# Hashing half of the next batch's pairs with products on GpSimd and sums on VectorE instead of matmuls on TensorE

## The chip, the cores and the metric

The kernel runs on one core of a Trainium2 chip (trn2). The metric is the device time of one execution in microseconds, the median of several runs. The engines are called as in the profile: PE (TensorE), DVE (VectorE), ACT (ScalarE), POOL (GpSimd) and SP (SyncE, which here only issues DMAs).

## The reference, cut to what matters

Two layers follow each other. The first is attention in which a query sees only the keys of the same hash bucket; the bucket is given by the signs of six projections.

```python
# q, k, v: (4, 8, 768, 64) float32; proj: (64, 6)
q_bits = (einsum('bhsd,dk->bhsk', q, proj) > 0)          # likewise k_bits
q_bucket = sum(q_bits * 2 ** arange(6)); k_bucket = ...
scores = where(q_bucket[..., :, None] == k_bucket[..., None, :], q @ k.T / 8, -1e9)
attn = softmax(scores) @ v                               # then heads side by side: x, 3072 x 512
# the second layer
ffn = (gelu(x @ w_gate) * (x @ w_val)) @ w_out           # 512 -> 1536 -> 512
out = x + sigmoid(x @ w_res) * ffn
```

## The kernel before, in words

There are four batches, and in each eight heads, taken as four pairs (`p` counts pairs, 0 to 15; `side` 0 is the query, 1 the key; `hi` is the head within the pair). A batch passes through two stages. In the **attention loop** a pair has 9 chunks, so a batch has 36 slots. A slot `s` issues the scores of one chunk on PE (`scores`, L407), their exponential on ACT (L412), some matmuls of the MLP's second half of the batch before (`mlp_mm`: `rps` L458, `fps` L472), and the product with the values of the chunk two slots earlier (`values`, L381). In the **gate stage** (`gate_val`) there are twelve blocks `m`; in each, 8 matmuls for the gate and 8 for the value (L426) fill two PSUM tiles `sp` from a ring of two; ACT takes the Gelu of the first (L445) and DVE multiplies it into the second (`hh`, L446).

The mask is folded into the matmul of the scores: each row of q and k, cast to bf16 by POOL into a tile `nat` (`cast`, L184 and L186), gets its six sign bits as further columns (`bits`, L225), and a DMA transpose on SP's queue brings the whole into the layout of the matmul (`turn`, L274, tile `aug`). There are only four `nat` tiles, so a cast waits for the `turn` of the tile's last user. To find the bits, DVE transposes the raw data in 32x32 blocks into a tile `t32` (`tr`, L194), PE multiplies them by the projection (`hash_mm`, L206, float32; 16 matmuls for two pairs, in four column groups), and DVE turns the sums back into rows of tokens (`hash_tok`, L216) before the bits are set.

An output tile `av` (PSUM, ring of two, one for each head) is opened by a DVE memset of a spare row (`opened`, L347), then a PE matmul puts a small multiple of the sum of all values there (`preset`, L355, which reads `vsum` from POOL's `vals_s`, L307 to L311), and a copy spreads that row over the six others (`repeat`, L359, DVE), after which `values` may add to it. When a head is done, DVE divides by the sum (`finish`, L332 and L333), which also frees the tile for `opened` of the pair after it. The MLP's output takes two DVE operations: L476 on `fps`, and L479, which adds x (`o` and `x_tok`, both in SBUF).

All order is written out by hand; every engine executes its own instructions in the order in which the program issues them. Batch 0 has a list, `ORDER`. In batches 1 to 3, `at(s, ...)` hangs a piece behind the values of slot `s`, `pe(s, ...)` behind its scores, and `gv(b, m, ...)` behind block `m` of batch `b`'s gate stage. Beside batch `b` the pairs of batch `b + 1` are prepared: the first two, called `xs`, and the second two, `ys`, each as four (pair, side) items. Both are hashed by PE in the gate stage: `xs` behind block 0, `ys` behind block 6, with DVE's `hash_tok` and `bits` behind blocks 0 to 4 and 7 to 10. Batch 0 prepares the pairs of batch 1 in the same way from `ORDER`.

Of the kernel before, what the change touches and what calls it, by code (L numbers as in the profile page):

```python
# [9 lines left out]
FP32 = mybir.dt.float32  # L10
BF16 = mybir.dt.bfloat16
AF = mybir.ActivationFunctionType
ALU = mybir.AluOpType
# [4 lines left out]
def kernel(  # L18
# [12 lines left out]
    nc = tc.nc  # L31
# [27 lines left out]
    ld_pool = ctx.enter_context(tc.tile_pool(name="ld", bufs=4))  # L59
    ldv_pool = ctx.enter_context(tc.tile_pool(name="ldv", bufs=3))  # L60
    aug_pool = ctx.enter_context(tc.tile_pool(name="aug", bufs=4))
    t32_pool = ctx.enter_context(tc.tile_pool(name="t32", bufs=6))
    va_pool = ctx.enter_context(tc.tile_pool(name="va", bufs=4))
    e_pool = ctx.enter_context(tc.tile_pool(name="e", bufs=4))
    sm_pool = ctx.enter_context(tc.tile_pool(name="sm", bufs=2))
    sc_ps = ctx.enter_context(tc.tile_pool(name="sc_ps", bufs=2, space=PSUM))
    av_ps = ctx.enter_context(tc.tile_pool(name="av_ps", bufs=2, space=PSUM))
# [105 lines left out]
    def nat_of(x):  # L173
        return nat[(2 * x[0] + x[1]) % NN]

    def cast(p, side, eng, h0=0, h1=2):
        x = (p, side)
        scale = (1.0 / C) if side == 0 else 1.0
        sl = slice(h0 * T, h1 * T)
        dst = nat_of(x)[:, sl, 0:D]  # L180
        if eng is nc.scalar:
            nc.scalar.activation(dst, raw[x][:, sl], AF.Copy, scale=scale)
        elif side == 0:
            eng.tensor_scalar(dst, raw[x][:, sl], scale, 1.0, op0=ALU.mult, op1=ALU.mult)  # L184
        else:
            eng.tensor_copy(dst, raw[x][:, sl])  # L186

    t32, hsum, htok = {}, {}, {}

    def tr(p, side, h0=0, h1=2):  # L190
        if (p, side) not in t32:
            t32[p, side] = t32_pool.tile([P, HT, 2, 32], FP32, tag="t32", name="t32")
        sl = slice(h0 * T, h1 * T)
        nc.vector.transpose(t32[p, side][:, sl].rearrange("p c h n -> p (c h n)"),  # L194
                            raw[p, side][:, sl].rearrange("p c d -> p (c d)"))
# [48 lines left out]
                                hs[:, 1, :, 0:NBITS], 0.0, 0.5, op0=ALU.is_gt, op1=ALU.subtract)  # L244


    def hash_heads(p, dh):
        if p not in hsum:
            hsum[p] = mm_ps.tile([P, T, 32], FP32, tag="r", name="hsh")
        hs = hsum[p]  # L250
        for j in range(4):
            hi, side = divmod(j, 2)
            nc.tensor.matmul(hs[32 * j:32 * j + 32], projw[:, dh, :],  # L253
                             t32[p, side][:, hi * T:hi * T + T, dh, :],
                             start=(dh == 0), stop=(dh == 1), tile_position=(0, 32 * j))

    def tok_heads(p):
        ht = sm_pool.tile([P, T, 32], FP32, tag="hth", name="hth")
        nc.vector.transpose(ht.rearrange("p c n -> p (c n)"),
                            hsum.pop(p).rearrange("p c n -> p (c n)"))  # L260
        htok[p] = ht
# [80 lines left out]
    def opened(p, hi):  # L342
        if (p, hi) in av:
            return
        av[p, hi] = av_ps.tile([P, T + 1, D + 1], FP32, tag="av", name="av")
        if p >= HP:
            nc.vector.memset(av[p, hi][:, T, :], 0.0)  # L347

    def preset(p, hi):
        o, w = av[p, hi], vsums[p][:, hi, 0:D + 1]  # L350
        if p < HP:
            nc.tensor.matmul(o[:, 0:T, :], eps_sb, w.unsqueeze(1).to_broadcast([P, T, D + 1]),  # L352
                             start=False, stop=True, skip_group_check=True)
        else:
            nc.tensor.matmul(o[:, T, :], eps_sb, w, start=False, stop=True, skip_group_check=True)  # L355

    def repeat(p, hi):
        o = av[p, hi]
        nc.vector.tensor_copy(o[:, 0:T, :], o[:, T:T + 1, :].to_broadcast([P, T, D + 1]))  # L359

    def x_turn(b, hp):
        pt = mm_ps.tile([P, T, P], BF16, tag="f", name="pt") if b == 0 else \
# [130 lines left out]
    def at(s, *pieces):  # L493
        side_work.setdefault(s, []).extend(pieces)

    def pe(s, *pieces):
        side_pe.setdefault(s, []).extend(pieces)

    def gv(b, m, *pieces):
        gv_work.setdefault((b, m), []).extend(pieces)  # L500

    def loads(s, *xs):
        for p, what in xs:
            at(s, (lambda p=p: load_v(p)) if what == "v" else
               (lambda p=p, w=what: load(p, "qk".index(w))))


    for p in range(HP, NPAIR):
        for hi, s in enumerate((9 * p - 1, 9 * p + 4)):
            if p == HP and hi == 0:  # L510
                gv(0, 8, lambda: opened(HP, 0))
                gv(0, 9, lambda: preset(HP, 0))
                gv(0, 9, lambda: repeat(HP, 0))
                continue
            at(s - 2, lambda p=p, hi=hi: opened(p, hi))
            pe(s, lambda p=p, hi=hi: preset(p, hi))
            at(s, lambda p=p, hi=hi: repeat(p, hi))

    def hashed(ps, i0=0, i1=4):
        jobs = [(p, side) for p in ps for side in range(2)]  # L520
# [73 lines left out]
    def lay(b, m, x):  # L594
        gv(b, m, lambda: bits(*x), lambda: turn(*x))

    for b in range(B - 1):
        s0, p0 = b * NSLOT, (b + 1) * HP
        xs = [(p0 + i, side) for i in range(2) for side in range(2)]
        ys = [(p0 + 2 + i, side) for i in range(2) for side in range(2)]  # L600
        for j, (x, y) in enumerate(zip(xs, ys)):
            if b == 0:
                for z in (x, y):
                    n = "%d%s" % (z[0], "qk"[z[1]])
                    put("ld " + n, lambda z=z: load(*z))
                    put("tr " + n, lambda z=z: tr(*z))
                n = "%d%s" % (x[0], "qk"[x[1]])
                put("cast " + n, lambda x=x: cast(*x, nc.gpsimd))
                put("hash 4.%d" % j, lambda p0=p0, j=j: hashed((p0, p0 + 1), j, j + 1))
                continue  # L610
            at(s0 + 24 + 2 * j, lambda x=x: tr(*x))
            at(s0 + 25 + 2 * j, lambda x=x: cast(*x, nc.gpsimd))
            if j < 2:
                at(s0 + 32 + 2 * j, lambda y=y: tr(*y))
            loads(s0 + 2 + 4 * j, (x[0], "qk"[x[1]]))
            loads(s0 + 18 + 3 * j, (y[0], "qk"[y[1]]))
        if b > 0:
            gv(b, 0, lambda p0=p0: hashed((p0, p0 + 1)))
        gv(b, 0, lambda p0=p0: tokens((p0, p0 + 1), True))
        for m, x in zip((0, 1, 2, 4), xs):  # L620
            lay(b, m, x)
        if b > 0:
            gv(b, 3, lambda y=ys[2]: tr(*y))
            gv(b, 5, lambda y=ys[3]: tr(*y))
        for m, y in zip((5, 5, 6, 6), ys):
            gv(b, m, lambda y=y: cast(*y, nc.gpsimd))
        if b > 0:
            gv(b, 6, lambda p0=p0: hashed((p0 + 2, p0 + 3)))
        gv(b, 7, lambda p0=p0: tokens((p0 + 2, p0 + 3), True))
        for m, y in zip((7, 8, 9, 10), ys):  # L630
            lay(b, m, y)
    for p in range(HP, NPAIR):
        at(9 * p - 8, lambda p=p: vals_s(p), lambda p=p: vals_a(p))
        loads(9 * p - 20, (p, "v"))

    mlp, done = [], [0]
    NMM = T * (KM + KF)
# [134 lines left out]
```

## Time and profile before

| | us |
|---|---|
| median of 3 runs (lowest to highest) | 344.25 (344.13 to 345.43) |
| the profiled execution's own time | 344.05 |
| its span, first to last instruction | 342.3 |
| PE busy | 337.0 (98%) |
| ACT busy | 208.1 (61%) |
| DVE busy | 192.9 (56%) |
| POOL busy | 86.1 (25%) |

A row of the groups by line gives line, engine, operation, output<-input tile, shapes and count, then the busy time and the mean duration of one in ns, then the idle time of the engine just before, with what ended it. The timeline gives start, duration, engine and line. The granted TensorE clock is full in all 40 slices.

Batch 1's gate stage runs from 126.4 to 160.7 us, batch 2's from 206.7 to 241.0, batch 3's from 286.7 to 317.9; between them lie the attention loops of batches 2 and 3.

### The profile page before, as it was taken

The page shows a single profiled execution, that of the slowest core. Times are in us where ns is not written, and L with a number is a line of the kernel's source. Part 1 is how long each engine was busy: PE and PEld are TensorE (multiplying, and loading weights), DVE is VectorE, ACT ScalarE, POOL GpSimd, SP SyncE. Part 2 cuts the span into 40 slices and gives each one's busy share as a digit, 9 for nine tenths or more (in the row PEclk, how much of TensorE's full clock was granted, in tenths as well). Part 3 has the DMA queues.
Part 4 walks back from the last instruction along what each step waited for, and adds up shares of the span by engine and source line. Part 5 has one row for each costly group of instructions (what it writes and reads, how often), then busy time and mean ns, then how long its engine had stood idle before and what let it go on. Part 6 is the DMA issues. An engine that isn't in the chain of part 4 may idle for free.

```text
span 342.3 us, 7633 instructions
## 1 busy us (share of the span) xinstructions
PE 337.0 (98%) x3124; PEld 204.6 (60%) x3124; DVE 192.9 (56%) x406; ACT 208.1 (61%) x235; POOL 86.1 (25%) x165
## 2 busy tenths in 40 slices
PE   8999999999999999999999999999999999999995
PEld 5667665665666665655666665656566665665443
DVE  6878847574444876756344775747334444333343
ACT  4889973237999862325999991222999994322220
POOL 3899830370055000170054000242030000000000
PEclk9999999999999999999999999999999999999999
DMA  7979999979386523518467542725431221000012
GB/s 225 377 153 231 308 184 183 162 114 208 123 186 191 159 77 90 110 19 166 105 164 213 181 107 69 132 49 103 82 97 36 56 56 61 3 0 0 33 61 93
DMA packets 69571, 42.50 MB, mean 124 GB/s; under 512 B 47904, under 2 KB 66592, under 8 KB 69536
## 3 DMA queue, kind: packets, MB, share of 16 engines
q1 hardware_dynamic: 63120, 36.77, 42.5%
q0 software_dynamic: 6336, 5.24, 10.6%
q8 instruction: 24, 0.39, 0.5%
q14 instruction: 11, 0.09, 0.1%
q10 hardware_dynamic: 80, 0.00, 0.0%
HBM read 29.36 MB, written 6.29 MB: 104 GB/s over the span
## 4 chain that ended last, share of the span: by engine, by line
PE 94%; ACT 3%; DMA 1%; DVE 1%; issue 0%; SPq 0%; DVEq 0%; ACTq 0%
PE sp L426 37%; PE fps L472 18%; PE sp L407 17%; PE av L381 10%; PE rps L458 6%; PE hs L206 3%; ACT e L412 3%; PE pt L285 1%; DMA ld<-in_q_dram 1%; PE pt L365 1%; PE hs L235 0%; PE av L352 0%; PE hsh L253 0%; PE av L355 0%; DVE o L479 0%
## 5 line engine op out<-in xcount | busy, mean ns | idle before, releaser
L412 ACT ACTIVATE e<-sp 128x1024 bf16<-128x1024 f32 x144 | 143.6, 1026 | 13.1 <-PE sp L407 8.4
L445 ACT ACTIVATE gt<-sp 128x768 bf16<-128x768 f32 x48 | 38.9, 811 | 93.6 <-PE sp L426 93.6
L407 PE MATMUL sp<-aug,aug 71*128 71x256 bf16 (+1 forms) x384 | 85.8, 325 | 0.3 <-ACT e L412 0.2
L472 PE MATMUL fps<-wo,hh 128*128 128x512 bf16 (+2 forms) x300 | 79.3, 370 | 0.0
L446 DVE TENSOR_TENSOR hh<-gt,sp 128x768 bf16<-128x768 bf16 x48 | 45.8, 955 | 52.1 <-PE sp L426 50.0
L426 PE MATMUL sp<-x_sb,wg 128*128 128x512 bf16 (+1 forms) x384 | 70.5, 326 | 0.1
L426 PE MATMUL sp<-x_sb,wv 128*128 128x512 bf16 (+1 forms) x384 | 70.4, 326 | 0.0
L381 PEld LDWEIGHTS <-e 128*128 128x128 bf16 x1152 | 52.7, 97 | 28.9 <-issue 1.2
L381 PE MATMUL av<-va,e 128*128 128x65 bf16 x1152 | 57.6, 193 | 0.0
L426 PEld LDWEIGHTS <-wg 128*128 128x128 bf16 x384 | 37.0, 98 | 26.0 <-issue 1.8
L426 PEld LDWEIGHTS <-wv 128*128 128x128 bf16 x384 | 37.6, 98 | 24.8
L472 PEld LDWEIGHTS <-hh 128*128 128x128 bf16 x300 | 27.5, 97 | 23.2
L407 PEld LDWEIGHTS <-aug 71*128 71x128 bf16 x384 | 29.4, 97 | 10.9 <-issue 1.4
L194 DVE STREAM_TRANSPOSE t<-ld 128x768 f32<-128x768 f32 (+1 forms) x34 | 30.7, 913 | 4.1 <-DMA ld<-in_q_dram 2.2
L307 POOL TENSOR_TENSOR v<-ldv 128x384 f32<-128x384 f32 x16 | 15.9, 996 | 66.5 <-DMA ldv<-in_v_dram 66.5
L184 POOL TENSOR_SCALAR nat<-ld 128x768 bf16<-128x768 f32 x15 | 12.4, 829 | 73.5 <-DMA aug<-nat 73.5
L476 DVE SCALAR_TENSOR_TENSOR o<-th,fps 128x512 f32<-128x512 f32 (+2 forms) x25 | 16.6, 666 | 24.5 <-PE fps L472 20.1
L458 PE MATMUL rps<-wr,x_sb 128*128 128x512 bf16 x96 | 28.1, 378 | 0.0
L332 DVE RECIPROCAL rec<-av 128x6 f32<-128x6 f32 x32 | 6.2, 193 | 32.9 <-PE av L381 31.0
L359 DVE COPY av<-av 128x390 f32<-128x390 f32 x24 | 13.6, 565 | 19.3 <-PE av L355 19.2
L462 ACT ACTIVATE th<-rps 128x512 f32<-128x512 f32 x24 | 14.2, 593 | 16.5 <-PE rps L458 16.5
L225 DVE TENSOR_SCALAR nat<-htp 32x72 bf16<-32x72 f32 x96 | 21.9, 229 | 1.7
(67 smaller groups left out, 209.5 us busy)
## 6 DMA issues: line engine op xcount, KB each, us to landing
ldv<-in_v_dram SPq DMA_DIRECT2D x16, 384.0 KB, 5.1
out_dram<-o SPq DMA_DIRECT2D x23, 256.0 KB, 2.1
ld<-in_q_dram SPq DMA_DIRECT2D x15, 384.0 KB, 5.1
ld<-in_k_dram SPq DMA_DIRECT2D x15, 384.0 KB, 4.5
wg<-in_moe_w_gate_dram POOLq DMA_DIRECT2D x4, 384.0 KB, 6.8
wv<-in_moe_w_val_dram POOLq DMA_DIRECT2D x4, 384.0 KB, 6.8
wo<-in_moe_w_out_dram POOLq DMA_DIRECT2D x3, 512.0 KB, 6.1
wr<-in_moe_w_res_dram POOLq DMA_DIRECT2D x1, 512.0 KB, 11.6
```

The costliest lines, as they stand in the source:

```text
L194: nc.vector.transpose(t32[p, side][:, sl].rearrange("p c h n -> p (c h n)"), raw[p, side][:, sl].rearrange("p c d -> p (c d)"))
L225: engs[a % len(engs)].tensor_scalar(nat_of(x)[32 * a:32 * a + 32, :, D:D + NBITS], ht[32 * j:32 * j + 32, :, NBITS * a:NBITS * (a + 1)], 0 ...
L307: nc.gpsimd.tensor_add(v3, vs[:, :, 0:3, :], vs[:, :, 3:6, :])
L381: nc.tensor.matmul(av[p, hi][:, qt, :], e[:, off:off + P], va[:, hi, jt, 0:D + 1], start=first, stop=(p >= HP and jt == T - 1), skip_group ...
L407: nc.tensor.matmul(sp[:, off:off + nq * P], ks[0:KA, hi * T + jt, :], qs[0:KA, hi * T + qt0:hi * T + qt0 + nq, :], start=True, stop=True)
L412: nc.scalar.activation(e, sp, AF.Exp, scale=float(ALPHA))
L426: nc.tensor.matmul(sp[:, c0:c1], w[:, kk, bass.ts(m, P)], xs[:, kk, c0:c1], start=(kk == 0), stop=(kk == KM - 1))
L445: nc.scalar.activation(gt, sp[:, 0:S], AF.Gelu)
L446: nc.vector.tensor_mul(hh[:, m, :], gt, ps[1][:, 0:S])
L458: nc.tensor.matmul(rps, x_sb[b][:, kk, t, :], wr[:, kk, :], start=(kk == 0), stop=(kk == KM - 1))
L472: nc.tensor.matmul(fps[:, cs], hh[:, m, bass.ts(t, P)], wo[:, m, cs], start=(m == 0), stop=(m == KF - 1))
L476: nc.vector.scalar_tensor_tensor(o[:, cs], th[:, cs], 1.0, fps[:, cs], op0=ALU.add, op1=ALU.mult)
```

## The change

Beside batches 1 and 2, the `ys` are no longer hashed by PE. For each of the four items, POOL forms the products of two token columns with all six projection vectors in one instruction (`multiply`, output 128 x 2 x 6 x 64, float32, both inputs read with a repeated dimension), and DVE sums each over the 64 (`add_up`, a reduction from 768 numbers to 12 in each partition). Six such pairs make one item; `bits_val` then sets its bits in one DVE instruction. The products take a ring of two tiles (`t2`) out of the six that `t32` had. The projection is spread once over all partitions (`spread_proj`). `tr`, `hash_mm`, `hash_tok` and four `bits` for each of these items go.

Two of the eight `repeat` copies of a batch (`(p % 4, hi)` of `(0, 0)` and `(2, 0)`) move from DVE to ACT. The pieces beside batches 1 to 3 have new places from a table `PLACE`: a whole part below 36 is a slot, 36 to 47 a gate block, 48 and above a slot of the batch after; a fraction below .5 means behind the scores (as `pe`), from .5 on behind the values (as `at`). Batch 0's own order stays, except for which `t32` tile each transpose writes (`TRING`).

```diff
-    t32_pool = ctx.enter_context(tc.tile_pool(name="t32", bufs=6))
+    t32_pool = ctx.enter_context(tc.tile_pool(name="t32", bufs=2))
+    TRING = (0, 1, 2, 0, 1, 2, 1, 0, 0, 1, None, None, 0, 1)
-            t32[p, side] = t32_pool.tile([P, HT, 2, 32], FP32, tag="t32", name="t32")
+            t32[p, side] = t32_pool.tile([P, HT, 2, 32], FP32, tag="t%d" % TRING[p], name="t32")
+    def spread_proj():
+        pb = sm_pool.tile([P, D, NBITS], FP32, tag="ht", name="pb")
+        nc.sync.dma_start(pb, proj.partition_broadcast(P))
+        nc.gpsimd.tensor_copy(projt, pb.rearrange("p d n -> p n d"))
+    def multiply(x, t):
+        pr = t32_pool.tile([P, 2, NBITS, D], FP32, tag="t2", name="pr")
+        nc.gpsimd.tensor_tensor(pr, raw[x][:, t:t + 2].unsqueeze(2).to_broadcast([P, 2, NBITS, D]),
+                                projt.unsqueeze(1).to_broadcast([P, 2, NBITS, D]), op=ALU.mult)
+        prod[x, t] = pr
+    def add_up(x, t):
...
+        nc.vector.tensor_reduce(hval[x][:, t:t + 2, :], prod.pop((x, t)),
+                                axis=mybir.AxisListType.X, op=ALU.add)
+    def bits_val(x):
+        nc.vector.tensor_scalar(nat_of(x)[:, :, D:D + NBITS], hval.pop(x), 0.0, 0.5,
+                                op0=ALU.is_gt, op1=ALU.subtract)
     def repeat(p, hi):
+        if (p % HP, hi) in ((0, 0), (2, 0)):
+            nc.scalar.activation(o[:, 0:T, :], o[:, T:T + 1, :].to_broadcast([P, T, D + 1]), AF.Copy)
+    PLACE = {
...
+        "tr x": (14.5, 26.02, 15.5, 25.04),
+        "cast x": (23.54, 6.04, 23.02, 25.5),
+        "bits x": (36.56, 36.6, 45.5, 37.52),
+        "turn x": (39.54, 37.5, 47.52, 44.58),
+        "cast y": (46.52, 38.52, 50.06, 62.02),
+        "bits y": (43.5, 43.54, 56.54, 70.06),
+        "turn y": (56.02, 47.5, 59.04, 70.52),
+        "mul y0": (22.04, 23.52, 31.02, 33.02, 33.5, 35.5),
+        "mul y1": (36.58, 38.5, 39.5, 41.5, 41.54, 42.52),
+        "mul y2": (42.54, 44.52, 49.02, 49.5, 50.04, 51.5),
+        "mul y3": (53.02, 57.02, 57.5, 58.5, 59.5, 61.52),
+        "add y0": (24.02, 29.5, 32.02, 33.06, 35.02, 37.54),
+        "add y1": (38.54, 39.52, 40.5, 41.52, 42.5, 43.52),
+        "add y2": (44.5, 46.5, 49.52, 50.02, 52.5, 53.5),
+        "add y3": (56.5, 57.52, 59.06, 61.5, 64.04, 67.02),
+        "open 0": (36.52, 7.02, 15.52, 25.02),
+        "open 1": (0.04, 11.02, 19.5, 29.02),
+        "preset 0": (44.56, 8.56, 18.04, 27.04),
+        "repeat 0": (46.54, 8.58, 18.5, 28.02),
+        "repeat 1": (5.04, 12.5, 23.04, 33.04),
...
     for b in range(B - 1):
...
-        if b > 0:
-            gv(b, 6, lambda p0=p0: hashed((p0 + 2, p0 + 3)))
```

## The prediction, made before the changed kernel was run

> **What bounds the kernel now.** First the page: its busy times, then the chain that ended last.
>
> ```profile
> PE 337.0 (98%) x3124; PEld 204.6 (60%) x3124; DVE 192.9 (56%) x406; ACT 208.1 (61%) x235; POOL 86.1 (25%) x165
> ...
> PE 94%; ACT 3%; DMA 1%; DVE 1%; issue 0%; SPq 0%; DVEq 0%; ACTq 0%
> ```
>
> PE is the bound almost everywhere; POOL has three quarters of its time free. Next the same chain in order of time, where the change acts:
>
> ```profile
> 126.43 2.60 PE sp L426 x16
> 129.03 1.44 PE hs L206 x32
> 130.47 15.71 PE sp L426 x96
> 146.18 1.44 PE hs L206 x32
> 147.61 13.11 PE sp L426 x80
> ```
>
> From 126.43 to 160.72 PE has no gap, and each hash is 1.44 us on the path (129.03 to 130.47, 146.18 to 147.61). Batch 2 has the same at 209.28 and 226.42. The groups kept apart by shape give the prices of what comes and goes:
>
> ```profile
> L194 DVE STREAM_TRANSPOSE t<-ld 128x768 f32<-128x768 f32 x30 | 28.6, 960 | 2.9 <-PE hs L206 1.9 <-DMA ld<-in_q_dram 1.0
> ...
> L479 DVE SCALAR_TENSOR_TENSOR o<-o,x_tok 128x512 f32<-128x512 f32 x23 | 17.1, 745 | 0.8
> ...
> L307 POOL TENSOR_TENSOR v<-ldv 128x384 f32<-128x384 f32 x16 | 15.9, 996 | 66.5 <-DMA ldv<-in_v_dram 66.5
> ...
> L309 POOL TENSOR_TENSOR v<-v 128x128 f32<-128x128 f32 x16 | 7.3, 454 | 1.3
> ```
>
> Last the timeline of POOL and of DVE at 177 us, for what the two do to each other:
>
> ```profile
> 177.25 0.83 POOL L184 TENSOR_SCALAR nat<-ld 128x768 bf16<-128x768 f32 x1
> ...
> 177.33 1.29 DVE L479 SCALAR_TENSOR_TENSOR o<-o,x_tok 128x512 f32<-128x512 f32 x1
> ...
> 178.03 1.27 POOL L186 CAST nat<-ld 128x768 bf16<-128x768 f32 x1
> ```
>
> L479 takes 0.69 us when POOL is quiet; here it began inside POOL's 0.83 and took 1.29, and POOL's next cast took 1.27 in place of 0.82. They took turns. Of all DVE groups only L479, with both inputs in SBUF, is ever stretched so: L446 stays at 0.95 and L194 at 0.97 beside a busy POOL.
>
> **What it removes.** Two hashes of 1.44 us, both on the path: 2.88 us. From DVE, beside each of the two batches, four transposes of 0.96 (two in late slots, two in gate blocks), one `hash_tok` of 0.59 and sixteen `bits` of 0.23; none held PE, so that is worth nothing by itself.
>
> **What it adds.** 48 products on POOL. The two rows of L307 and L309 lie on a line of (0.996 - 0.454) / 256 = 2.12 ns an element; 768 elements are 0.454 + 640 x 0.00212 = 1.81 us. Nearest rows on both sides: the cast L299, one input of 768, 0.85 us, is the floor. The 32x72 `bits` on POOL (L225, twelve short runs) takes 0.469, 0.23 more than the casts' line gives for 72 elements (0.50 for 384, 0.83 for 768), so 19 ns a run; with that for some 10 to 20 more runs a product would be 2.0 to 2.2. I take 1.8, since L307 is the same operation with two inputs. All 48 are 87 us, spread over two batch times of some 77 us.
>
> 48 sums on DVE. No reduction is in the trace. The nearest are L194 and L446, 768 elements in 0.96, some 0.88 from start to start when nothing is waited for; below, 0.69 (L476, 512 elements); above, 1.29 (L479 when it waits for POOL). I take 0.95, 46 us in all, where 20 go (16.2 of the hash, 3.4 of six copies).
>
> The Trainium skill (GPSIMD Engine Reference, "Performance versus the Vector engine") speaks against the change: elementwise work with two inputs belongs on VectorE, which is about twice as fast. The trace agrees in size: L479's slope between 128x128 (0.292) and 128x512 (0.69 undisturbed) is 1.04 ns an element, half of POOL's 2.12. By the rule the products would go to DVE at 0.292 + 640 x 0.00104 = 0.96 each, 23 us more of DVE in each batch; as the walk below shows, DVE has not that much left, so the rule does not decide here.
>
> Six `repeat` copies go from DVE (0.57) to ACT, about 0.5 each (L367, 256 columns, 0.38; L462, 512, 0.59). ACT is busy 25.0 of 27.0 us in the first slots of batch 2, and one copy there still fits; a slip of under 0.9 us of an exponential is hidden by the second `sp` tile. `spread_proj` is one DMA and one POOL copy (0.5 to 1.0) where POOL sat idle 16.4 us: nothing. If that cover were gone, 1.0 us of POOL.
>
> In batch 0 the transpose of 6q now waits for the hash of 4q, which is read until 44.2: DVE does it at 44.25 where it did it at 41.39, so 7k and 6k come 0.96 later. What follows is head (3,1)'s division, before which DVE sat idle 1.02 us for PE. Covered; otherwise up to 1.0.
>
> **The waits it adds.** Every sum waits on DVE for its product, and behind it wait `hh`, `finish`, `opened` and `repeat`, on which PE waits; every third product waits on POOL for a sum (ring of two), and behind it wait casts and the sums of the values.
>
> *Gate blocks* (2.60 us each). DVE: `hh` 0.95 and one sum 0.95, at most another 0.95 of `bits` (block 1): 2.85, less two overlaps of 0.08: 2.7. PE needs `hh`'s tile again after the next gate half, so the slack is 1.30 - 0.95 = 0.35: held. POOL: 8 products in the stage, 14.5, two casts, `vals` 3.0: 19 of 31 us. The cast behind the second product waits for the `turn` issued behind block 1: bits done at 133.0, landing 3.7 later, 136.7; POOL arrives at 137.7. Covered by 1.0.
>
> *Slots 0 to 22 of the batch after* are the tight stretch: DVE has there 10 sums 9.5, L476 and L479 thrice 4.2, four divisions 3.0, two transposes 1.9, copies and memsets 2.2: 20.8 of 26.5 us. I walk it from the end of block 11. Sums 2 and 3 of item y2 end at 2.7; product 4 started when sum 2 had freed its tile, 2.0, and ends 3.8; sum 4 ends 4.7; `repeat` 5.2. POOL: cast 3.7 to 4.5, product 5 to 6.2, y3's first to 8.0. L476 runs at 6.9, when `fps` is complete; L479 could start at 7.6 and takes its turn after the product, until 8.5. Sum 5 until 9.4, division 10.1, memset for (9,0) 10.3. PE reaches that `preset` at 10.6: slack 0.3. The same way on: three more sums, L479 again waiting for a product until 17.8, sum 18.7, transpose, division, transpose, memset for (10,0) 21.3; PE wants it at 21.6: slack 0.3. POOL's sum of values for pair 11 comes at 31.1, wanted 32.1; the `repeat` for (11,0) 34.7, wanted 34.8.
>
> So with these prices nothing stops PE, but slacks of 0.1 to 0.3 us after eight products in a row will not all hold: I allow 0.4 for both batches together. Sum against the profiled execution: 344.05 - 2.88 + 0.4 = 341.6. That execution lies 0.2 under the median of the runs.
>
> **The rivals.** *Part of it is given back* (0.22): a product of 1.9 to 2.05. The memset at slot 18 comes after some eight products in turn, so each 0.1 makes it 0.8 later, less 0.3 of slack, in two batches: 1.9 to 2.05 costs about 1.0 to 3.4, and gives 342.2 to 344.6. For it: the two inputs are read in up to twelve runs. Against: L307's straight line has the same start, 0.18, as the casts, which have twelve runs of 64.
>
> *POOL becomes the bound* (0.20, the slower side). At 2.2 a product the memset of slot 18 comes 8 x 0.4 - 0.3 = 2.9 late in each of two batches, and POOL's queue to pair 11's sum of values (11 products) costs another 1.5 in batch 2: 344.05 - 2.88 + 7.3 = 348.5. It decides from about 2.1 us a product (2 x (2.4 - 0.3) + 0.5 = 4.7, less 2.88). The same would come of sums that take turns with the products as L479 does, at once some 0.5 each. Against: L194, one input from SBUF, is never stretched.
>
> *The matmuls' time is not freed*, since PE then waits for `hh`: block 7 would start 1.44 sooner, but DVE also loses `hash_tok` there. I see no more than 0.1 in it, so it gets no chance of its own.
>
> **How the numbers follow.** The main case, 0.58, has 341.0 to 342.4. About 0.5% (1.7 us) is what a measurement of this kernel can tell from no change; faster by that is below 342.5. Taking in the first rival and half of the second, the range is 340.8 to 346.0. Faster 0.58, same 0.22, slower 0.20.
>
> **What would show it.** L206 with 160 records, not 224; gate stages of batches 1 and 2 of 32.9 us, not 34.3; a POOL row of 48 tensor-tensors near 1.8, POOL near 175 us busy; a DVE row of 48 reductions near 0.95; L479's mean up to about 0.85. Right would be that the attention loops of batches 2 and 3 keep their length within 0.5. Wrong would be products of 2.1 or more, reductions stretched beside POOL, or PE idle before L355 or L381 in those loops, waiting for DVE's memset or copy.

## The result, and the profile after

The changed kernel takes 342.73 us (median of 4 runs, 342.28 to 342.96) against 344.50 for the kernel before beside it (4 runs, 344.13 to 345.43): a ratio of 0.9943, 95% interval 0.9919 to 0.9967. It is faster by 0.57%, little more than the 0.5% that the prediction gives as what can be told from no change. Its profiled execution took 342.96 us, span 341.3.

From the page of the kernel after, its busy times, the engines' shares of the chain that ended last, and three groups:

```profile
PE 332.9 (98%) x3014; PEld 203.5 (60%) x3060; DVE 221.1 (65%) x414; ACT 210.0 (62%) x241; POOL 174.5 (51%) x214
...
PE 90%; DVE 4%; ACT 3%; issue 2%; POOL 0%; DVEq 0%; ACTq 0%; POOLq 0%
...
L259 POOL TENSOR_TENSOR pr<-ld,projt 128x768 f32<-128x768 f32 x48 | 86.4, 1811 | 41.2 <-DVE hv L266 41.0
...
L266 DVE TENSOR_REDUCE hv<-pr 128x12 f32<-128x768 f32 x48 | 44.6, 936 | 4.7 <-POOL pr L259 4.6
...
L509 DVE SCALAR_TENSOR_TENSOR o<-o,x_tok 128x512 f32<-128x512 f32 (+2 forms) x25 | 22.3, 894 | 0.9
```

A product takes 1.811 us and a sum 0.936. PE is still 98% busy, but DVE's share of the chain is 4% where it was 1%: somewhere DVE has become what PE waits for. L509 is the old L479 (L506 is L476, L476 is L446, L208 is L206, L374 and L382 are `opened` and `preset`).

Where the time went is read best by stage. The table is worked out from the start times in PE's timeline. "Start" is the beginning of the first hash in the last quarter of batch 0's attention loop. A gate stage runs from its first matmul to the first `rps` of the loop that follows it, a loop from there to the next gate stage. Loops 2 and 3 follow the gate stages of batches 1 and 2; loop 1 is the one before.

| profile of | start | loop 1 | gate 1 | loop 2 | gate 2 | loop 3 | gate 3 | span |
|---|---|---|---|---|---|---|---|---|
| before | 39.87 | 45.37 | 34.72 | 45.52 | 34.73 | 45.33 | 31.20 | 342.3 |
| after | 40.41 | 45.47 | 33.57 | 45.86 | 33.57 | 45.64 | 31.20 | 341.3 |
| e4, no products or sums | 40.41 | 45.34 | 33.21 | 45.34 | 33.21 | 45.34 | 31.21 | 339.6 |
| e1, bits and turn moved | 40.40 | 45.47 | 33.21 | 47.03 | 33.21 | 45.70 | 31.20 | 342.2 |
| e2, a sum later | 40.43 | 45.47 | 33.57 | 46.70 | 33.58 | 45.78 | 31.20 | 342.3 |
| e3, write-back into PSUM | 40.45 | 45.35 | 33.57 | 45.34 | 33.57 | 45.34 | 31.20 | 340.4 |
| e5, slower products | 39.66 | 45.47 | 33.57 | 47.25 | 33.58 | 45.92 | 31.21 | 342.2 |
| e6, copies on DVE | 39.94 | 45.35 | 33.57 | 45.85 | 33.57 | 45.63 | 31.20 | 340.6 |
| e7, products on DVE | 39.78 | 46.35 | 36.67 | 54.09 | 36.17 | 49.60 | 31.20 | 359.4 |
| e8, bits moved alone | 39.71 | 45.46 | 33.21 | 45.86 | 33.22 | 45.63 | 31.20 | 339.8 |
| e9, e3 and e8 | 40.71 | 45.35 | 33.21 | 45.34 | 33.21 | 45.34 | 31.20 | 339.9 |
| e10, before with e3's edit | 40.68 | 45.37 | 34.72 | 45.37 | 34.72 | 45.33 | 31.20 | 343.0 |
| before, second profile | 40.72 | 45.43 | 34.72 | 45.78 | 34.72 | 45.34 | 31.20 | 343.5 |

From before to after the two gate stages lose 1.15 and 1.16 us, the three loops grow by 0.10, 0.34 and 0.31: 1.56 less in all. The start differs by 0.54 the other way, so the spans show only 1.0; the medians show 1.77. The second profile of the kernel before (last row) has loop 2 at 45.78 instead of 45.52. Against that one the loops grow by 0.04, 0.08 and 0.30, and the stages lose 1.88 in all. The medians lie between the two. The row without products is the floor: 33.21 for a gate stage and 45.34 for a loop. So the change leaves two things on the table: 0.36 in each gate stage, and 0.13, 0.52 and 0.30 in the loops.

**The gate stage.** The chain of the kernel after, in order of time:

```profile
129.67 1.44 PE hs L208 x32
...
133.92 0.95 DVE hh L476
...
136.91 0.96 DVE hh L476
...
137.92 2.11 PE sp L456 x12
```

The one hash that is left stands alone; behind it PE's run of blocks breaks off, and the chain goes through DVE, from one `hh` to the next. DVE's timeline there, in the kernel after (start, duration, what, and in brackets the idle time before with its releaser):

```profile
133.92 0.95 DVE L476 TENSOR_TENSOR hh<-gt,sp 128x768 bf16<-128x768 bf16 x1 [0.22 <-PE sp L456]
134.91 0.98 DVE L227 TENSOR_SCALAR nat<-htp 32x72 bf16<-32x72 f32 x4
135.92 0.95 DVE L266 TENSOR_REDUCE hv<-pr 128x12 f32<-128x768 f32 x1
136.91 0.95 DVE L476 TENSOR_TENSOR hh<-gt,sp 128x768 bf16<-128x768 bf16 x1
137.78 0.94 DVE L266 TENSOR_REDUCE hv<-pr 128x12 f32<-128x768 f32 x1
```

Block 1 has `hh`, four `bits` and a sum, one behind the other with no time between them: 2.99 us from `hh` to `hh`, where a block of PE is 2.60. PE's timeline shows what it costs:

```profile
136.25 1.46 PE L456 MATMUL sp<-x_sb,wg 128*128 128x512 bf16 x8
137.92 1.46 PE L456 MATMUL sp<-x_sb,wv 128*128 128x512 bf16 x8 [0.20 <-DVE hh L476]
```

Eight matmuls take 1.30 from start to start when nothing waits; here it is 1.67, so 0.37 are lost.

**The loops.** Loops 2 and 3 run level with the kernel before up to slot 8 and then lose 0.30 at slot 9, at the `preset` of head (9,0) or (13,0). DVE's timeline of the kernel after, ahead of it:

```profile
167.14 0.69 DVE L506 SCALAR_TENSOR_TENSOR o<-th,fps 128x512 f32<-128x512 f32 x1 [1.58 <-ACT e L442]
167.86 1.13 DVE L509 SCALAR_TENSOR_TENSOR o<-o,x_tok 128x512 f32<-128x512 f32 x1
168.91 0.94 DVE L266 TENSOR_REDUCE hv<-pr 128x12 f32<-128x768 f32 x1
...
170.63 0.11 DVE L374 MEMSET av<- 128x65 f32 x1
```

and POOL's, at the same time:

```profile
164.85 3.58 POOL L259 TENSOR_TENSOR pr<-ld,projt 128x768 f32<-128x768 f32 x2
```

L509 could have begun to work at 167.86 and been done in 0.69; it waits for the second product, which ends at 168.43, and takes 1.13. Everything behind it up to the memset (L374) shifts with it. PE has this in its timeline of the kernel after:

```profile
170.43 0.41 PE L411 MATMUL av<-va,e 128*128 128x65 bf16 x8
...
171.02 0.59 PE L437 MATMUL sp<-aug,aug 71*128 71x512 bf16 x2
```

From the values (L411) to the next scores (L437) it is 0.59 us, with the `preset` between them. The view of PE's waits does not list this one; only the comparison with a run that lacks it (e3 below: 0.27) shows it.

In loop 2 another 0.22 go in slot 29, where the values of head (11,0) wait for its copy (L389). The chain of the kernel after, in order of time, passes through DVE there:

```profile
193.65 1.15 DVE o L509
194.80 0.49 DVE av L389
```

It is L509 again, 1.15 us long, this time beside POOL's casts and not beside a product. 0.30 and 0.22 are loop 2's 0.52 above the floor; loop 3 has the 0.30 alone.

Loop 1 loses 0.12 at the same slot, but not by L509, which takes its 0.69 there. L506 ahead of it begins late: 32.51 us after the start of the loop, where it is 32.15 in e4. What held it the profile does not show. The late start is also in loop 1 of e1, e2, e5 and e8, and it is missing from loop 1 of e3, e4, e6 and e9.

### The profile page after: what moved, and what is told of

It reads as the page before. It is cut to its first block, busy times and chain, and to the rows that moved or that the text cites. A ratio compares the mean times of both kernels' runs of the same rounds, so it can differ in the third digit from the quotient of the medians.

```text
span 341.3 us, 7515 instructions
## 1 busy us (share of the span) xinstructions
PE 332.9 (98%) x3014; PEld 203.5 (60%) x3060; DVE 221.1 (65%) x414; ACT 210.0 (62%) x241; POOL 174.5 (51%) x214
## 4 chain that ended last, share of the span: by engine, by line
PE 90%; DVE 4%; ACT 3%; issue 2%; POOL 0%; DVEq 0%; ACTq 0%; POOLq 0%
PE sp L456 34%; PE fps L502 17%; PE sp L437 17%; PE av L411 10%; PE rps L488 6%; ACT e L442 3%; PE hs L208 2%; PE hs L237 1%; DVE hh L476 1%; PE wps L151 1%; PE pt L312 1%; DVE o L509 1%; DVE nat L227 1%; PE pt L395 1%; DVE t L196 1%
## 5 line engine op out<-in xcount | busy, mean ns | idle before, releaser
L259 POOL TENSOR_TENSOR pr<-ld,projt 128x768 f32<-128x768 f32 x48 | 86.4, 1811 | 41.2 <-DVE hv L266 41.0
L437 PE MATMUL sp<-aug,aug 71*128 71x256 bf16 (+1 forms) x384 | 85.8, 325 | 0.4 <-ACT e L442 0.2
L476 DVE TENSOR_TENSOR hh<-gt,sp 128x768 bf16<-128x768 bf16 x48 | 45.8, 954 | 46.1 <-PE sp L456 44.0
L502 PE MATMUL fps<-wo,hh 128*128 128x512 bf16 (+2 forms) x278 | 74.6, 369 | 1.1
L456 PE MATMUL sp<-x_sb,wv 128*128 128x256 bf16 (+1 forms) x374 | 69.9, 324 | 0.9 <-DVE hh L476 0.4
L456 PE MATMUL sp<-x_sb,wg 128*128 128x256 bf16 (+1 forms) x376 | 70.0, 325 | 0.5
L411 PEld LDWEIGHTS <-e 128*128 128x128 bf16 x1152 | 52.7, 97 | 29.3 <-issue 1.8
L411 PE MATMUL av<-va,e 128*128 128x65 bf16 x1152 | 57.6, 193 | 0.1
L266 DVE TENSOR_REDUCE hv<-pr 128x12 f32<-128x768 f32 x48 | 44.6, 936 | 4.7 <-POOL pr L259 4.6
L437 PEld LDWEIGHTS <-aug 71*128 71x128 bf16 x384 | 29.4, 97 | 11.1 <-issue 1.7
L506 DVE SCALAR_TENSOR_TENSOR o<-th,fps 128x512 f32<-128x512 f32 (+2 forms) x25 | 16.6, 666 | 25.2 <-PE fps L502 17.1
L488 PE MATMUL rps<-wr,x_sb 128*128 128x512 bf16 x90 | 26.4, 378 | 0.4
L196 DVE STREAM_TRANSPOSE t<-ld 128x768 f32<-128x768 f32 (+1 forms) x26 | 22.7, 895 | 4.3 <-PE hs L208 2.7
L509 DVE SCALAR_TENSOR_TENSOR o<-o,x_tok 128x512 f32<-128x512 f32 (+2 forms) x25 | 22.3, 894 | 0.9
L185 POOL TENSOR_SCALAR nat<-ld 128x768 bf16<-128x768 f32 x15 | 13.7, 911 | 14.7 <-DMA aug<-nat 14.7
L187 POOL CAST nat<-ld 128x768 bf16<-128x768 f32 (+1 forms) x15 | 12.9, 862 | 13.9 <-DMA aug<-nat 6.8
```

The lines of the kernel that those rows point to most:

```text
L259: nc.gpsimd.tensor_tensor(pr, raw[x][:, t:t + 2].unsqueeze(2).to_broadcast([P, 2, NBITS, D]), projt.unsqueeze(1).to_broadcast([P, 2, NBITS ...
L266: nc.vector.tensor_reduce(hval[x][:, t:t + 2, :], prod.pop((x, t)), axis=mybir.AxisListType.X, op=ALU.add)
L411: nc.tensor.matmul(av[p, hi][:, qt, :], e[:, off:off + P], va[:, hi, jt, 0:D + 1], start=first, stop=(p >= HP and jt == T - 1), skip_group ...
L437: nc.tensor.matmul(sp[:, off:off + nq * P], ks[0:KA, hi * T + jt, :], qs[0:KA, hi * T + qt0:hi * T + qt0 + nq, :], start=True, stop=True)
L456: nc.tensor.matmul(sp[:, c0:c1], w[:, kk, bass.ts(m, P)], xs[:, kk, c0:c1], start=(kk == 0), stop=(kk == KM - 1))
L476: nc.vector.tensor_mul(hh[:, m, :], gt, ps[1][:, 0:S])
```

## The experiments

Theory: the hash is gone from the path in full, products and sums have the predicted lengths, and what is given back are two waits for DVE, each with one cause: block 1 of the gate stages is overfull, and L509 takes turns with POOL at the tight places of the loops. Rivals: POOL itself is the bound; a cost at the start; the moved copies.

**e4: what the change costs in all.** `multiply` and `add_up` return at once, and the signs come from a tile of zeros.

```diff
     def multiply(x, t):
+        return
...
     def add_up(x, t):
+        hval[x] = hzero
+        return
```

> Leaves out all 48 products and 48 sums (the signs of these four items are set from a tile of zeros); the places, the copies on ACT and the missing hashes are the changed kernel's. Theory (all that is lost of the 2.88 us is DVE's and POOL's added work): the gate stages are 33.27, the loops of batches 2 and 3 as long as before or shorter, and the time is about 2.9 us under the kernel before, near 341.5. Rival (the new places or the copies on ACT cost something by themselves): it stays above 342.2.

Measured: 340.86 us (340.54 to 341.32), ratio 0.990 (0.9882 to 0.9918). This is the floor row of the table. One hash is worth 34.72 - 33.21 = 1.51 us of the path (its row has 1.44), and the products and sums cost 342.73 - 340.86 = 1.9 us together by the medians, 1.67 by the stages.

**e1: emptying block 1, with the turn.** Two of the four `bits` of item x3 go from block 1 to block 9, and its `turn` from block 8 to block 9.

```diff
-        "bits x": (36.56, 36.6, 45.5, 37.52),
-        "turn x": (39.54, 37.5, 47.52, 44.58),
+        "bits x": (36.56, 36.6, 45.5, 37.52, 45.54),
+        "turn x": (39.54, 37.5, 47.52, 45.58),
...
+                place(b, "bits x", 3, lambda x=x: bits_half(*x, 0))
+                place(b, "bits x", 4, lambda x=x: bits_half(*x, 1))
```

> Half of the bits of one item (the first two pairs' last key) move from behind gate block 1 to behind block 9, so that DVE has there half a set of bits and a sum. Theory (the gate stages of batches 1 and 2 lose 0.30 us each because hh, four bits and a sum take 2.99 us behind block 1): each of these gate stages goes from 33.57 to about 33.27 us, the hash's 1.44 us less than before in full; the attention loops keep 45.86 and 45.64; the run is about 0.6 us under the changed kernel, near 342.1. Rival (the 0.30 us comes from something other than DVE's row there): the gate stages keep 33.57.

Measured: 343.83 us (343.17 to 344.02), ratio 0.9978 (0.9969 to 0.9988), 1.1 slower than the changed kernel. The gate stages do fall to 33.21. But loop 2 is 47.03: at slot 9 it loses 1.2 us more than the kernel after. POOL's timeline and DVE's in this run:

```profile
164.87 0.83 POOL L185 TENSOR_SCALAR nat<-ld 128x768 bf16<-128x768 f32 x1 [1.15 <-DMA aug<-nat]
```

```profile
167.50 2.30 DVE L517 SCALAR_TENSOR_TENSOR o<-o,x_tok 128x512 f32<-128x512 f32 x1
```

The later `turn` keeps a `nat` tile longer; POOL's cast waits 1.15 us for it, the two products behind the cast end at 169.25 instead of 168.43, and the add with x (L517 here) waits for both of them: 2.30 us. The block was the cause of the gate stall, and the edit brought a second effect with it. So it was done again without the `turn`. (In the cuts of both edits, `bits_half` sets two of an item's four `bits`.)

**e8: emptying block 1, without the turn.** The two `bits` go from block 1 to block 2.

```diff
-        "bits x": (36.56, 36.6, 45.5, 37.52),
+        "bits x": (36.56, 36.6, 45.5, 37.52, 38.53),
...
+                place(b, "bits x", 3, lambda x=x: bits_half(*x, 0))
+                place(b, "bits x", 4, lambda x=x: bits_half(*x, 1))
```

> Half of item x3's bits moves from gate block 1 to gate block 2; its turn stays where it is (in e1_split_bits it went one block later, and POOL's cast behind it then waited 1.15 us more). The rest is the changed kernel. Theory: block 1's stall of 0.36 goes, gate stages 33.21 in place of 33.57, and the chain to slot 9 runs along with PE (hh paces the sums), so loops 2 and 3 stay at 45.9 and 45.6 within 0.15: 342.73 - 0.7 = 342.0. Rival (the chain to slot 9 is paced by POOL's products, not by PE): what the gate stage gains, the memset of slot 9 gives back, loops 46.2 and 46.0, time 342.7.

Measured: 341.84 us (341.56 to 342.05), ratio 0.9913 (0.9898 to 0.9927). DVE's timeline in the same block:

```profile
133.23 0.95 DVE L484 TENSOR_TENSOR hh<-gt,sp 128x768 bf16<-128x768 bf16 x1 [0.22 <-PE sp L464]
...
135.83 0.95 DVE L484 TENSOR_TENSOR hh<-gt,sp 128x768 bf16<-128x768 bf16 x1
```

From `hh` to `hh` it is 2.60, the gate stages are 33.21 and 33.22, and the loops stay as they were. The rival, that the memset of slot 9 would give the gain back, fell: the sums behind `hh` move along with PE.

**e2: one sum out of the way of slot 9.**

```diff
-        "add y2": (44.5, 46.5, 49.52, 50.02, 52.5, 53.5),
+        "add y2": (44.5, 46.5, 49.52, 50.02, 52.5, 55.04),
```

> The sum that stands on DVE ahead of the division and the memset for the second pair's first head moves behind that memset. Theory (the attention loops of batches 2 and 3 lose 0.30 us at slot 9 because that memset comes too late): the memset comes 0.9 us sooner, PE waits at slot 9 no more, the loops go from 45.86 and 45.64 to about 45.55 and 45.35; but the product that waits for the moved sum, and all after it, come up to 1.2 us later, so that some may be lost again at slot 18. Rival (the loops are longer for another reason, such as the exponentials or the matmuls themselves): the stall at slot 9 goes or stays, and the loops keep their length.

Measured: 343.93 us (343.19 to 344.41), ratio 0.9985 (0.9974 to 0.9995). The wait at slot 9 is gone (0.31), and two others have come, at the `preset` of (9,1) and of (10,0). By the start times of the scores behind them they cost 0.45 and 0.68, so loop 2 is 0.84 longer than in the kernel after. The sum is not all that came later. DVE's timeline of this run, behind the memset of slot 9:

```profile
171.48 1.17 DVE L270 TENSOR_SCALAR nat<-hv 128x72 bf16<-128x72 f32 x1
```

In the kernel after this `bits_val` takes 0.33 there. Here the product behind the moved sum is later too (170.79 to 172.60), and `bits_val` lasts until that product ends, which costs DVE 0.84. How the loss divides between the moved sum and this second effect was not tried apart; shown is that moving one piece within the stretch from slot 9 to slot 18 was no remedy. In loop 3, where no next batch is prepared, the gain at slot 9 and the loss at the next `preset` leave 0.14.

**e3: L509 without its second SBUF input.** L506 writes its result back into its PSUM tile, and the add with x reads it there.

```diff
-                nc.vector.scalar_tensor_tensor(o[:, cs], th[:, cs], 1.0, fps[:, cs],
+                nc.vector.scalar_tensor_tensor(fps[:, cs], th[:, cs], 1.0, fps[:, cs],
...
-                nc.vector.scalar_tensor_tensor(o3, o3, 0.5, x_tok[b][:, k0:k1, t, :],
+                f3 = fps[:, cs].rearrange("p (k n) -> p k n", n=P)
+                nc.vector.scalar_tensor_tensor(o3, f3, 0.5, x_tok[b][:, k0:k1, t, :],
```

> The MLP's first DVE operation writes back into its PSUM tile and the second reads it from there, so that the second has one input in SBUF instead of two; everything else is the changed kernel's. Theory (L509 takes turns with POOL's products because both its inputs are in SBUF, and that is what makes the memset for slot 9 late): the second operation's mean goes from 0.935 to about 0.70, none is stretched beside a product, the loops of batches 2 and 3 lose nothing at slot 9 and go to about 45.55 and 45.35; the gate stages keep 33.57; about 0.6 us less. Rival (any DVE operation that reads SBUF beside a product is stretched): the mean stays above 0.85 and the loops keep their length.

Measured: 342.07 us (341.73 to 342.27), ratio 0.9933 (0.9913 to 0.9953). All three loops are at the floor (45.35, 45.34, 45.34) with the products still there; loop 1 is there in e6 too, without this edit, so its 0.12 is not counted for it. DVE's timeline before slot 9, the groups by shape, and PE's timeline at slot 9 in this run:

```profile
167.78 0.69 DVE L510 SCALAR_TENSOR_TENSOR o<-fps,x_tok 128x512 f32<-128x512 f32 x1
```

```profile
L510 DVE SCALAR_TENSOR_TENSOR o<-fps,x_tok 128x512 f32<-128x512 f32 x23 | 15.9, 691 | 0.8
```

```profile
170.35 0.41 PE L411 MATMUL av<-va,e 128*128 128x65 bf16 x8
...
170.62 0.60 PE L437 MATMUL sp<-aug,aug 71*128 71x512 bf16 x2
```

The same add at the same place, beside the same products, takes 0.69 instead of 1.13; all 23 have a mean of 0.691, where L509's 512-wide form has 0.935 in the kernel after. From L411 to L437 it is 0.27 instead of 0.59. The Trainium skill (SBUF — State Buffer, "Who interferes with whom") says that a VectorE instruction with two SBUF inputs contends with a GpSimd instruction that reads SBUF, under an exclusive lock, and that one with at most one SBUF input does not, outside the modes that use both ports. The two rows, 0.935 and 0.691, agree with it.

**e10: the same edit without products.** The kernel before, with e3's edit and nothing else.

> The kernel before with the write-back into PSUM of e3_psum_stt and nothing else: tells whether that edit gains by itself or only against the products. Theory (L509 is stretched by the products): the loops before stood at 45.37, 45.52 and 45.33 against 45.34 without products, so at most 0.2 to 0.3 is there to be had; the time stays within 0.4 of 344.5. Rival (a general gain of the edit): loop 2 and others shorter than 45.34, time 343.5 or less.

Measured: 344.27 us (343.75 to 344.90), ratio 0.9989 (0.9980 to 0.9999). Loop 2 goes from 45.52 to 45.37, and no other stage moves. What it mends there stands in DVE's timeline of the first profile of before, and then of the second:

```profile
185.60 0.99 DVE L479 SCALAR_TENSOR_TENSOR o<-o,x_tok 128x512 f32<-128x512 f32 x1
```

```profile
186.49 1.26 DVE L479 SCALAR_TENSOR_TENSOR o<-o,x_tok 128x512 f32<-128x512 f32 x1
```

L479 took turns with POOL's casts and sums of values ahead of the memset for (10,1) before the change too, and PE's scores behind it start 0.14 and 0.41 later than in e4. With the edit it takes 0.69 there. So the edit alone is worth 0.15 or 0.41 in these profiles and 0.4 in the medians, a tenth of a per cent. In the changed kernel this place costs nothing any more, and the edit takes away other waits: 0.30 in loop 3, which the kernel before does not lose at all, and 0.52 in loop 2. The 0.30 at slot 9 of each loop comes from the products; the 0.22 of slot 29 stands beside casts, at the new places.

**e5: slower products.** A memset of 128x128 on POOL ahead of each product.

```diff
+    idle = const.tile([P, P], BF16, name="idle")
...
     def multiply(x, t):
+        nc.gpsimd.memset(idle, 0.0)
```

> A memset of 128x128 (bf16, 0.15 to 0.25 us) goes on POOL ahead of each product; the products themselves stay. It tests the prediction's slope: each 0.1 us more of a product makes DVE's memset of slot 18 0.8 later in each of two loops. Theory (POOL's queue in the loops' first half has no slack left): with 0.2 more each, loops 2 and 3 grow from 45.9 and 45.6 by 1.2 to 1.6 each; with one queue less full in the gate stages nothing changes there (33.6); the time is 2.4 to 3.5 above the changed kernel's 342.7, so 345.0 to 346.3. Rival 1 (only the memset of slot 9 is late, the rest of the loop has slack as the profile before suggested): 0.4 to 0.6 in each loop, 343.5 to 344.0. Rival 2 (POOL waits for sums anyway, 41 us in all, and absorbs it): within 0.4 of 342.7.

Measured: 344.34 us (343.90 to 345.07), ratio 0.9993 (0.9984 to 1.0003); 1.6 above the changed kernel. By the timelines two products in a row start 1.92 apart here and 1.77 in the kernel after, so each comes 0.15 dearer. Loop 2 grows by 1.39, loop 3 by 0.28: the theory's size held in loop 2 alone, and the time lies between its range and the first rival's. PE's waits over the whole span (what waited, on what; us in total, times, longest), and DVE's timeline at the end of loop 2:

```profile
PE av L385 <- DVE av L377: 0.9, 3, 0.3
PE pt L398 <- DVE x_tok L363: 0.7, 1, 0.7
```

```profile
202.09 2.07 DVE L512 SCALAR_TENSOR_TENSOR o<-o,x_tok 128x512 f32<-128x512 f32 x1
```

Three waits for the memset are of about 0.3 each in this list; they lie at slots 9 and 18 of loop 2 and at slot 9 of loop 3. By start times, against the kernel after, they cost 0.29 more at each slot 9 and 0.43 at slot 18. The 0.7 is a new place: the last division of loop 2, behind an add with x that waited for a product for 1.4 us. POOL is busy there with the products of the next batch's item y0, which loop 3 does not have.

**e6: the six copies back on DVE.**

```diff
-        if (p % HP, hi) in ((0, 0), (2, 0)):
+        if False:
```

> All repeat copies go back to DVE, as in the kernel before; the rest is the changed kernel. It prices the part of the change that moves six copies to ACT. Theory (DVE is full from slot 0 to slot 22 and has room elsewhere): the copy of head (10,0) in slot 18 puts 0.5 more ahead of the division and memset that follow, so loops 2 and 3 grow by 0.2 to 0.6 each; the copy behind block 10 puts 0.5 ahead of the sums and the memset of slot 9: 0.2 to 0.5 more each; in all 0.8 to 2 above 342.7. Rival (the copies fit into DVE's waits for products, 41 us of such idle time on POOL's side and several of 0.5 to 1.6 on DVE's): within 0.4 of 342.7.

Measured: 342.33 us (342.02 to 342.90), ratio 0.9936 (0.9920 to 0.9953). The theory fell: the loops are 45.35, 45.85 and 45.63, as after or shorter. (In loop 2 the 0.2 of slot 29 stays although L509 takes only 0.79 there: L506 begins late, as in loop 1 of the kernel after.) The move to ACT was worth nothing; the copies fit between DVE's other work.

**e7: the products on DVE.** The other engine for the same 48 instructions.

```diff
-        nc.gpsimd.tensor_tensor(pr, raw[x]...
+        nc.vector.tensor_tensor(pr, raw[x]...
```

> The 48 products go on DVE in the same places, ahead of their sums there; the rest is the changed kernel. Theory of the prediction: each is about 0.96 us on DVE (both inputs in SBUF, float32), 46 us more, DVE about 263 us busy; the first 26.5 us of loops 2 and 3 have 20.8 of DVE's work already and get some 10 more products, 30.4 in all, so each loop grows by about 4, and gate blocks with hh, a product and a sum (2.86 of 2.60) by 0.25 to 0.6 each, about 1.5 to 2 a stage: 342.7 + 2 x 5.5 to 6 = 352 to 355. Rival (a product is half as long on DVE as on POOL, a sum then waits for nothing, and L509 finds POOL quiet and is back at 0.69): the loops go back to 45.3 and the time to 341 to 343.

Measured: 364.09 us (361.12 to 365.38), ratio 1.0579 (1.0545 to 1.0613). One group by shape and the largest of PE's waits:

```profile
L259 DVE TENSOR_TENSOR pr<-ld,projt 128x768 f32<-128x768 f32 x48 | 49.5, 1044 | 0.2
```

```profile
PE sp L456 <- DVE hh L476: 5.0, 9, 0.8
PE av L411 <- DVE av L389: 4.1, 2, 2.4
```

A product is 1.04 us there, not much more than half of POOL's 1.81, and the kernel is 21 us slower than with the slow ones: gate stages +3.1 and +2.6, loop 1 +0.9, loop 2 +8.2, loop 3 +4.0 (the profiled execution, 361.12, was the shortest of the four). The direction was the theory's, the size nearly twice its estimate, above all in loop 2.

**The start: the kernel before, once more.**

> The kernel before, unchanged, profiled a second time, for one question: in its first profile the first hash of batch 0's ninth last slot started at 39.87 us, in all five profiles of changed kernels at 40.40 to 40.45, though every engine's queue is the same up to about 15 us. Theory A (scatter of the first loads: k of pair 1 landed at 9.5 to 10.3 us in these profiles, and POOL's casts, sums of values and bits_head queue behind it): the start lies anywhere from 39.8 to 40.5, and one profile at 40.2 or more shows it. Theory B (a cost of the change, from the three pairs of t32 tiles or the places of batch 0): 39.87 again, within 0.1. Stages after that as in the first profile: gate stages 34.7, 34.7, 31.2, loops 45.3 to 45.5.

Measured: 345.25 us in its one run; the start lies at 40.72. POOL's timeline of the first profile of before, and then of the second:

```profile
14.11 3.16 POOL L266 TENSOR_SCALAR nat<-hth 32x36 bf16<-32x36 f32 x8
```

```profile
15.12 3.17 POOL L266 TENSOR_SCALAR nat<-hth 32x36 bf16<-32x36 f32 x8
```

The second time POOL reaches the bits of batch 0 a microsecond later, since its first casts waited longer for their loads, and PE waits 0.73. Over all profiles the start lies between 39.66 (e5) and 40.72 (this run), with and without the change. It is scatter of the first loads, and no cost of the change; the 0.54 between the profiles of before and after must be left out when they are compared. Two things were not as expected: 40.72 is beyond the 39.8 to 40.5, and loop 2 is 45.78, not 45.3 to 45.5, by the wait told under e10.

**e9: both mends together.** e8's split of the bits and e3's write-back.

> The split of e8_bits_block2 and the write-back into PSUM of e3_psum_stt together. Theory: gate stages 33.21, loops 45.34, as with no products at all in e4_no_products; that is 0.72 and 0.95 less than the changed kernel's profile, so 341.0 to 341.4, and about 0.991 of the kernel before. Rival (each mend frees an engine that the other one then fills): one of the two gains is lost, 341.7 to 342.1.

Measured: 341.28 us (340.89 to 341.66) against 344.66 beside it, ratio 0.9893 (0.9877 to 0.9910). Gate stages 33.21, loops 45.34 to 45.35: each is at the floor of the run without any product. This version beats both kernels; it takes 3.4 us off the kernel before, nearly twice what the change did.

## Why the prediction was right, and where it was off

The forecast was faster, 341.6 us, with 340.8 to 346.0 as the range; 342.73 lies in the range, 1.1 above the point. It was a near thing: 342.73 is above the main case (341.0 to 342.4) and above the 342.5 that the prediction set, from 344.25, as the bound of faster; against the 344.50 beside it the gain of 1.77 is just over its 1.7. It falls where the first rival was to lie (342.2 to 344.6), but that rival's cause, a dearer product, did not come. By its steps:

- **The hash.** Predicted 1.44 each. The floor gives 1.51, 3.02 for both, 0.14 better than the sum had it.
- **The product, the sum, the copies.** 1.8 predicted from the line through L307 and L309, 1.811 measured; the repeated dimensions of its inputs cost nothing. 0.95 predicted from rows of as many elements, 0.936 measured, the same beside a busy POOL (the rival of sums that take turns fell). ACT's copies were put at 0.5 and took 0.489, and by e6 they were worth nothing. POOL busy: 175 predicted, 174.5 measured. Neither rival of dearer products came about.
- **Batch 0.** "Covered" held: from the start to the first gate stage it is 6.58 us before and 6.59 after.
- **The gate blocks: the step that failed.** The prediction had 2.85 less two overlaps of 0.08, so 2.7, and a slack of 0.35: "held". Both terms were wrong, and the stage was not held. In the kernel after a sum begins 0.87 after the `hh` ahead of it (136.91 to 137.78), which is such an overlap; but `hh` behind a sum begins 0.99 after it, and `bits` 0.99 after `hh`. So the chain is 2.99. The trace before had the second of these: there too `bits` begins 0.99 after `hh` (133.28 to 134.27). And the slack left out how long `hh` takes to start: in an undisturbed block of the kernel before, DVE's and PE's timelines have

```profile
135.88 0.95 DVE L446 TENSOR_TENSOR hh<-gt,sp 128x768 bf16<-128x768 bf16 x1 [0.67 <-PE sp L426]
```

```profile
135.61 1.46 PE L426 MATMUL sp<-x_sb,wg 128*128 128x512 bf16 x8
136.91 1.46 PE L426 MATMUL sp<-x_sb,wv 128*128 128x512 bf16 x8
```

  `hh` begins 0.27 after PE turned to the next half (135.61), ends at 136.83, and PE takes the tile again at 136.91. The slack is 0.08, less the 0.05 or so between a DVE end and the matmul it releases (136.91 + 0.96 to 137.92 in the chain after): about 0.03. 2.99 - 2.60 - 0.03 = 0.36, which is what each stage lost (33.57 against 33.21). At 2.7 the block would already have cost 0.07. This was 0.72 of the miss. The prediction had named the mechanism among its rivals (PE waits for `hh`, so the matmuls' time is not freed), for block 7, and saw no more than 0.1 in it; it came in block 1.
- **The walk of the loops.** The memset for (9,0) was put 10.3 us after block 11's end, wanted at 10.6. Its row ends at 170.74, 10.53 after that end (160.21), and PE lost 0.3. The walk had the mechanism right, L509 behind the product; it put the product's end at 8.0, where it was 8.22, and L509's end at 8.5, where the next sum began at 8.70. PE wanted the memset some 0.3 before the walk's 10.6. A margin of 0.3 between two chains of ten instructions was no margin, and the one of 0.1 at the copy for (11,0) was none either: put at 34.7 and wanted at 34.8, it ended at 195.28, which is 35.1, and cost the 0.22. The other two held: the memset for (10,0) came at 21.6 with PE 0.3 later too, and pair 11's sum of values did not hold PE. By the prediction's own list PE idle before `preset` or `values`, waiting for the memset or the copy, was a sign of being wrong, and it came, at slots 9 and 29; what held is that the loops of batches 2 and 3 keep their length within 0.5. Against the first profile of before the three loops gave back 0.75 where 0.4 was allowed, against the second 0.42. The mean of L479, put at up to 0.85, became 0.935. "Of all DVE groups only L479" was a misreading of the trace before: its `bits` that read SBUF (L225 in batch 0) took 0.40 to 0.45 three times, at 28.71 beside POOL's L309, and 0.19 to 0.23 the other nine times.
- **The sum.** Predicted -2.88 + 0.4 = -2.48. Measured by stages: -3.02 + 0.72 + 0.75 = -1.55, or -1.88 with the second profile of before.
- **The rivals' slope.** "Each 0.1 makes it 0.8 later, in two batches" was half right. For the 0.15 of e5 it gives 2 x (8 x 0.15 - 0.3) = 1.8, and the two loops grew by 1.67 together; but that is luck. It was 1.39 in loop 2 and 0.28 in loop 3, and of the 1.39 only 0.43 came at the memset of slot 18. Loop 3 costs less than its half; beside batch 3 no next batch is prepared.
- **The rule that spoke against the change.** The rule of the Trainium skill (GPSIMD Engine Reference, "Performance versus the Vector engine") on elementwise work with two inputs has the direction right (1.04 on DVE, 1.81 on POOL: a ratio of 1.7 where it says about two), and the prediction's reason for setting it aside, that DVE had no room left, is what e7 showed: 21 us.

## What to carry to other kernels

An engine that is 56% busy on average can still have one block of 2.6 us that is full: count each block's queue without overlaps, and take the slack from two rows (the end of the last reader, the start of the next writer), not from the difference of durations. Before putting work that reads SBUF on GpSimd, look on VectorE for operations with two SBUF inputs and give them one in PSUM: here that edit was worth 0.15 to 0.41 us of loop time without the products and 0.82 with them. And when a piece is moved to make room, ask what moves with it: much the same mend cost 1.1 us with its DMA transpose and gained 0.9 without it.

## What had not been expected of the hardware

VectorE's small `bits_val` (L270, one SBUF input, 128x72, float32 to bf16) also takes turns with POOL. It takes 0.20 to 0.34 at six of its eight places in the kernel after, and 0.45 at one; at the last, DVE's and POOL's timelines have

```profile
186.76 0.82 DVE L270 TENSOR_SCALAR nat<-hv 128x72 bf16<-128x72 f32 x1
```

```profile
186.30 1.23 POOL L185 TENSOR_SCALAR nat<-ld 128x768 bf16<-128x768 f32 x1
```

`bits_val` ends as the cast does (187.58 and 187.53), 0.5 later than alone, and in e2 it lasted 1.17, until a product ended. The cast's own 0.4 more fit the L509 ahead of `bits_val`, which ran until 186.84. The Trainium skill (SBUF — State Buffer, "Who interferes with whom") has this too: it counts `tensor_scalar` among the operations that can enter a mode with both ports and then contend. The prediction had looked for turns among L479, L446 and L194 only. The 32-row `bits` (L227), as small and of the same types, read PSUM and stood at 0.23 to 0.24 throughout the gate block shown.

Why DVE's overlap of about 0.1 between neighbouring instructions fails in block 1 was not tried; shown is only that it is absent from the sum to `hh` and from `hh` to `bits` (0.99 each) and present from `hh` to the sum (0.87).
